# Softmax row sums on VectorE over a pair of heads, and one head of a pair normalised on ScalarE

## The chip, the core and the metric

The kernel runs on one core of a Trainium2 chip. The core has five engines that run their own instruction queues in order and wait for each other by semaphores: TensorE (PE; its weight loads are listed as PEld), VectorE (DVE), ScalarE (ACT), GpSimd (POOL) and SyncE (SP), which here issues nearly all DMAs. The metric is the device time of one execution in microseconds. Three runs of the kernel before took 858.59, 859.97 and 860.6 us; the median is 859.97.

## The reference

Attention feeds two feed-forward layers, all in float32.

```python
def _attn_ref(q, k, v):                       # (4, 8, 576, 64)
    scores = scale * np.matmul(q, k.transpose(0, 1, 3, 2))
    # heads 0-3 see the last 32 keys, heads 4-7 every 32nd key, both causal
    scores = np.where(masks[None, :, :, :], scores, -1e9)
    scores = scores - np.max(scores, axis=-1, keepdims=True)
    attn = np.exp(scores)
    attn = attn / (np.sum(attn, axis=-1, keepdims=True) + 1e-09)
    return np.matmul(attn, v)
# _moe_ref:  h = x @ w_in;  g = s * relu(h)**2 + b;  x = g @ w_out     (2304 x 512 x 2048)
# _moe2_ref: h = x @ w_in;  g = h * cos(h);          x = g @ w_out
```

## The kernel before, in words

**Attention.** The heads of a batch are taken in pairs. A batch has five pairs: two of local heads (kind "loc"), two of strided heads ("str"), and one ("rem") that holds the rows left over from all of them. With four batches there are 20 pairs of two items each, 40 items. A local item has its scores in one PSUM bank as 128 rows by 4 blocks of 96 columns, a strided item as 126 by 4 blocks of 126; a rem item has one block of 96 and two of 72. Softmax runs per row and block, so the statistics of an item are 4 columns (or 1 and 2) of a small tile `sm`: row 0 the negated maximum, row 1 the sum, row 2 its reciprocal. `part` is one large SBUF array; a ring of six pieces of 512 columns in it holds the exponentials p and the transposed p.

For a pair `run_scores` issues the score matmuls, then by a generator: `mask_max` for each item (in batches 0 and 1 PE adds the mask, `PE_MASK = 2`; later VectorE adds it, line 431, and the scores then lie in SBUF), `exps` (line 449: one ACTIVATE per block with a per-row bias, and with `accum_out`, which leaves the row sum), and `norm` on VectorE (lines 462 to 464: add 1e-9, reciprocal, multiply). Each ACTIVATE with `accum_out` shows in the trace as two instructions, ACTIVATE and ACTIVATION_READ_ACCUMULATOR. `run_transp` then transposes p on PE and copies it out on ScalarE (line 482), `run_values` multiplies by V (line 552) and splits the result into a high part (ScalarE, line 133) and a low part (VectorE, line 136), `xhi` and `xlo`, which the first layer reads.

**Order.** The generators are advanced by `tick()`. Batch 0 is done first, with dummy matmuls filling PE (line 531) and weight conversion (lines 143 and 174 to 181 on VectorE, 141 on ScalarE, then the split in lines 133 and 136) between. Then the slots of the first layer run, 20 slots of 512 (or 256) tokens by 4 feature blocks to a pass, and the attention of batches 1 to 3 is issued between them at rates of 0.5 and 0.3 steps to a group of matmuls. A scheduler then places each engine's instructions by their priority and by when it expects their operands. A slot needs the `xhi` and `xlo` of its tokens. The second layer follows, then the output.

Of the kernel before, what the change touches and what calls it, by code (L numbers as in the profile page):

```python
# [103 lines left out]
def net(ctx, tc, qk, rqk, vloc, vstr, rv, w1, w2, s, b, out):  # L104
# [270 lines left out]
    class Item:  # L375


        def __init__(self, bb, hp, j, kind):
# [45 lines left out]
        def mask_max(self, alloc):  # L424
            self.p = alloc()
            self.sm = sm_p.tile([P, 3, 4], F32, tag="sm", name="sm")
            for i, (m, k, n, c, mask) in enumerate(self.parts):
                src = self.view(self.s_ps, i)
                if not self.pe_mask:
                    dst = self.view(self.p, i)  # L430
                    nc.vector.tensor_tensor(dst, src, mask, ALU.add)  # L431
                    src = dst
                nc.vector.tensor_reduce(self.sm[:m, 0, i : i + n], src, axis=AX.X, op=ALU.max, negate=True)  # L433
                nc.vector.tensor_scalar(self.sm[:m, 0, i : i + n], self.sm[:m, 0, i : i + n], SCALE, None, ALU.mult)

# [21 lines left out]

        def norm(self):
            for i, (m, k, n, c, _) in enumerate(self.parts):
                dst = self.view(self.p, i)  # L460
                sm = self.sm[:m, :, i : i + n]
                nc.vector.tensor_scalar_add(sm[:, 1, :], sm[:, 1, :], 1e-9)
                nc.vector.reciprocal(sm[:, 2, :], sm[:, 1, :])
                normed[0] = nc.vector.tensor_tensor(  # L464
                    dst, dst, sm[:, 2, :].unsqueeze(2).to_broadcast([m, n, k]), ALU.mult
                )
# [765 lines left out]
```

## Time and profile before

| | |
|---|---|
| median of three runs | 859.97 us |
| span of the profiled execution, first to last instruction | 858.2 us |
| PE busy | 848.4 us, 99% |
| DVE busy | 594.5 us, 69% |
| ACT busy | 510.3 us, 59% |
| granted TensorE clock, mean | 0.999 of full speed |

For the profiled execution only its span is listed, no time of its own. Busy time of PE is not PE at its peak, since matmuls are pipelined and their ends are modelled. The 40 slices of the page show VectorE and ScalarE busy mainly in the first sixth of the span: the tenths of the first seven slices are 5, 9, 9, 8, 9, 9, 7 for DVE and 6, 8, 8, 9, 8, 9, 7 for ACT, and 3 to 8 thereafter. That sixth holds the attention.

### The profile page before, as it was taken

What the parts mean: (1) busy time and instruction counts of PE and PEld (TensorE: products, weight loads), DVE (VectorE), ACT (ScalarE), POOL (GpSimd) and SP (SyncE); (2) the same over time, 40 slices, a digit from 0 to 9 for tenths busy, and PEclk for the clock granted to TensorE, in tenths of its full rate; (3) what the DMA queues carried; (4) which work ended last, traced back from release to release, by engine and by line L of the source; (5) the groups of instructions that cost most, each with busy time, mean ns of one, the idle gap of its engine ahead of it and who ended that gap; (6) DMA issues with size and microseconds to landing.
All of it is one profiled execution on the core that took longest, in us unless ns stands there. A gap on an engine that the chain in (4) does not pass through costs nothing.

```text
span 858.2 us, 13480 instructions
## 1 busy us (share of the span) xinstructions
PE 848.4 (99%) x4901; PEld 724.5 (84%) x4901; DVE 594.5 (69%) x1269; ACT 510.3 (59%) x1121; POOL 4.0 (0%) x15
## 2 busy tenths in 40 slices
PE   9999999999999999999999999999999999999997
PEld 5667778898888888898888998998988989989886
DVE  5998997379867988597895476555665554644553
ACT  6889897466545765466564566455564554644543
POOL 1000000000000000000000000000000000000000
PEclk9999999999999999999999999999999999999999
DMA  9656551036434755277442765565664655755411
GB/s 282 192 168 181 161 162 50 1 129 202 166 117 147 234 183 175 108 262 254 153 155 86 240 207 179 183 210 172 238 215 160 220 164 183 277 175 189 166 50 75
DMA packets 65203, 147.40 MB, mean 172 GB/s; under 512 B 6272, under 2 KB 24960, under 8 KB 65136
## 3 DMA queue, kind: packets, MB, share of 16 engines
q1 hardware_dynamic: 64992, 146.40, 51.1%
q8 instruction: 39, 0.64, 0.3%
q14 instruction: 28, 0.23, 0.1%
q10 hardware_dynamic: 144, 0.13, 0.0%
HBM read 118.72 MB, written 27.79 MB: 171 GB/s over the span
## 4 chain that ended last, share of the span: by engine, by line
PE 90%; DVE 4%; ACT 4%; DMA 1%; issue 0%; SPq 0%; ACTq 0%
PE acc L1063 23%; PE acc L687 21%; PE h_ps L687 21%; PE pa L1125 10%; PE pb L1125 10%; ACT part L449 2%; PE t_ps L474 1%; PE o_ps L552 1%; DMA wraw<-in_w_dram 1%; PE s_ps L517 1%; DVE part L464 1%; ACT part L482 1%; PE dummy L786 1%; DVE sm L433 0%; ACT xhi L133 0%; DVE part L431 0%
## 5 line engine op out<-in xcount | busy, mean ns | idle before, releaser
L687 PE MATMUL h_ps<-xhi,w 128*128 128x512 f32 (+1 forms) x640 | 197.7, 372 | 0.8 <-ACT xhi L133 0.5
L687 PE MATMUL acc<-gh,w 128*128 128x512 f32 (+1 forms) x640 | 195.9, 370 | 0.0
L1063 PE MATMUL acc<-w2l,gh 128*128 128x512 f32 x576 | 177.7, 390 | 0.0
L687 PEld LDWEIGHTS h_ps<-xhi,w 128*128 128x128 f32 x640 | 116.8, 189 | 22.2 <-DVE w L136 1.0
L136 DVE TENSOR_TENSOR gl<-r,gh 128x512 fp32r<-128x512 f32 (+3 forms) x130 | 96.8, 745 | 53.7 <-ACT gh L998 40.4
L687 PEld LDWEIGHTS acc<-gh,w 128*128 128x128 f32 x640 | 117.0, 189 | 19.9 <-issue 0.2
L1063 PEld LDWEIGHTS acc<-w2l,gh 128*128 128x128 f32 x576 | 107.8, 188 | 21.6
L687 PE MATMUL acc<-gl,w 128*128 128x512 f32 (+1 forms) x320 | 118.5, 370 | 0.0
L687 PE MATMUL h_ps<-xlo,w 128*128 128x512 f32 (+1 forms) x320 | 118.4, 370 | 0.0
L1063 PE MATMUL acc<-w2l,gl 128*128 128x512 f32 x288 | 112.4, 391 | 0.0
L1125 PE MATMUL pa<-xhi,wfl 128*128 128x384 f32 x336 | 99.6, 337 | 0.0
L1125 PE MATMUL pb<-xhi,wfl 128*128 128x384 f32 x336 | 99.5, 336 | 0.0
L710 ACT ACTIVATE r<-h_ps 128x512 f32<-128x512 f32 (+1 forms) x80 | 44.4, 555 | 89.5 <-PE h_ps L687 89.3
L998 ACT ACTIVATE r<-h 128x768 f32<-128x768 f32 (+1 forms) x50 | 40.7, 816 | 95.3 <-DVE h L1111 95.1
L133 ACT ACTIVATE gh<-r 128x512 fp32r<-128x512 f32 (+1 forms) x80 | 47.1, 588 | 39.1 <-DVE r L716 38.7
L687 PEld LDWEIGHTS acc<-gl,w 128*128 128x128 f32 x320 | 60.4, 189 | 9.9
L687 PEld LDWEIGHTS h_ps<-xlo,w 128*128 128x128 f32 x320 | 60.4, 189 | 9.6
L1063 PEld LDWEIGHTS acc<-w2l,gl 128*128 128x128 f32 x288 | 54.1, 188 | 11.2
L1125 PEld LDWEIGHTS pa<-xhi,wfl 128*128 128x128 f32 x336 | 62.0, 188 | 1.7
L1125 PEld LDWEIGHTS pb<-xhi,wfl 128*128 128x128 f32 x336 | 61.9, 188 | 1.5
L1013 ACT ACTIVATE r<-r 128x768 f32<-128x768 f32 (+1 forms) x50 | 40.9, 820 | 32.1 <-DVE r L1011 32.1
L1011 DVE SCALAR_TENSOR_TENSOR r<-a,r 128x768 f32<-128x768 f32 (+1 forms) x50 | 46.2, 926 | 19.6 <-ACT a L998 19.4
(109 smaller groups left out, 1243.0 us busy)
## 6 DMA issues: line engine op xcount, KB each, us to landing
wfl<-wf SPq DMA_DIRECT2D x72, 512.0 KB, 4.9
w2l<-w2s SPq DMA_DIRECT2D x48, 512.0 KB, 3.2
wraw<-in_w_dram SPq DMA_DIRECT2D x56, 256.0 KB, 3.7
praw<-in_w_dram SPq DMA_DIRECT2D x32, 256.0 KB, 3.1
oraw<-in_w_dram SPq DMA_DIRECT2D x16, 512.0 KB, 3.7
wf<-ob SPq DMA_DIRECT2D x16, 512.0 KB, 3.5
w2s<-ow SPq DMA_DIRECT2D x16, 512.0 KB, 3.9
wfl<-wf SPq DMA_DIRECT2D x24, 256.0 KB, 4.1
```

Source lines behind the costliest of these rows:

```text
L133: nc.scalar.activation(dst_hi, src, AF.Copy)
L136: return nc.vector.tensor_tensor(dst_lo, src, hi.bitcast(F32), ALU.subtract)
L449: nc.scalar.activation(dst[:, t, :], src[:, t, :], AF.Exp, bias=self.sm[:m, 0, i + t : i + t + 1], scale=SCALE, accum_out=self.sm[:m, 1, i ...
L464: normed[0] = nc.vector.tensor_tensor(dst, dst, sm[:, 2, :].unsqueeze(2).to_broadcast([m, n, k]), ALU.mult)
L474: self.moves = nc.tensor.transpose(self.t_ps[:k, o : o + m], src[:, t, :], ident[:m, :m])
L687: nc.tensor.matmul(*args, **kw)
L710: relu[0] = nc.scalar.activation(r, h, AF.Relu)
L998: nc.scalar.activation(*args, **kw)
L1011: nc.vector.scalar_tensor_tensor(r, m, MAGIC, r, ALU.subtract, ALU.subtract)
L1013: nc.scalar.activation(r, r, AF.Sin, scale=-TWO_PI)
L1063: nc.tensor.matmul(accs[e], g[:, e * P : (e + 1) * P], w[:, wi, :], start=p == 0 and f == 0 and i == 0, stop=p == NPAIR - 1 and f == 1 and ...
L1125: nc.tensor.matmul(pb[bi], a, b[:, m, :], start=st and m == 0 and i == 0, stop=m == 1 and i == 2, skip_group_check=True)
```

## The change

`accum_out` goes from the exponentials. A new class `Softmax` works on one item ("half") or on both items of a pair, whose p now lie side by side in one piece of 1024 columns and whose statistics share one tile. In batch 0 each item is a half: its row sums come from a TENSOR_REDUCE on VectorE, and VectorE normalises both items as before. In batches 1 to 3 the pair is taken jointly: one maximum where VectorE has added the mask, one scaling, one sum, one addition of 1e-9 and one reciprocal for both items. Item 0 is then normalised on VectorE and item 1 on ScalarE, by one ACTIVATE (Copy with a per-row scale) per block, in one step of the generator later. The ring of pieces is 3 of 1024 columns instead of 6 of 512. The lines of the changed kernel are: 438 exponentials, 534 and 538 maxima, 536 mask, 539 scaling, 543 sums, 544 and 545 addition and reciprocal, 552 the multiplication on ScalarE, 559 that on VectorE, 458 the copy of the transposed p, 758 and 759 the first layer's activation (710 and 711 before).

```diff
@@ exps
                     nc.scalar.activation(
-                        dst[:, t, :],
-                        src[:, t, :],
-                        AF.Exp,
-                        bias=self.sm[:m, 0, i + t : i + t + 1],
-                        scale=SCALE,
-                        accum_out=self.sm[:m, 1, i + t : i + t + 1],
+                        dst[:, t, :], src[:, t, :], AF.Exp, bias=self.sm[:m, 0, i + t : i + t + 1], scale=SCALE
                     )
@@ tevac
-            self.pt = alloc()
+            if self.pt is None:
+                b = alloc()
+                self.pt, self.mate.pt = b[:, :512], b[:, 512:]
@@ new class Softmax
+        def maxima(self):
+            for i, (m, k, n, c, mask) in enumerate(self.parts):
+                for it in self.its:
+                    src = it.view(it.s_ps, i)
+                    if self.pe_mask:
+                        nc.vector.tensor_reduce(it.sm[:m, 0, i : i + n], src, axis=AX.X, op=ALU.max, negate=True)
+                    else:
+                        nc.vector.tensor_tensor(it.view(it.p, i), src, mask, ALU.add)
+                if not self.pe_mask:
+                    nc.vector.tensor_reduce(self.col(i, 0), self.view(i), axis=AX.X, op=ALU.max, negate=True)
+                nc.vector.tensor_scalar(self.col(i, 0), self.col(i, 0), SCALE, None, ALU.mult)
+
+        def sums(self):
+            for i in range(len(self.parts)):
+                nc.vector.tensor_reduce(self.col(i, 1), self.view(i), axis=AX.X, op=ALU.add)
+                nc.vector.tensor_scalar_add(self.col(i, 1), self.col(i, 1), 1e-9)
+                nc.vector.reciprocal(self.col(i, 2), self.col(i, 1))
+
+        def scaled(self, j):
+            it = self.its[j]
+            for i, (m, k, n, c, _) in enumerate(self.parts):
+                dst = it.view(it.p, i)
+                for t in range(n):
+                    nc.scalar.activation(dst[:, t, :], dst[:, t, :], AF.Copy, scale=it.sm[:m, 2, i + t : i + t + 1])
+            it.ready = True
+
+        def norm(self, j):
...
@@ run_scores
-        for it in pair:
-            it.mask_max(alloc)
+        p = alloc().rearrange("p (j c) -> p j c", j=2)
+        sm = sm_p.tile([P, 3, 8], F32, tag="sm", name="sm").rearrange("p r (j n) -> p r j n", j=2)
...
+        if pair[0].bb:
+            both = Softmax(pair, p, sm, 0, 2)
+            both.maxima()
+            yield
+            for it in pair:
+                it.exps()
+                yield
+            both.sums()
+            both.norm(0)
+            yield
+            both.scaled(1)
+            return
+        halves = [Softmax(pair, p, sm, j, j + 1) for j in range(2)]
+        for half in halves:
+            half.maxima()
         yield
         for it in pair:
             it.exps()
             yield
-        for it in pair:
-            it.norm()
-            it.ready = True
+        for half in halves:
+            half.sums()
+            half.norm(0)
@@ alloc
-            o = NP0 + (self.ni % NPB) * 512
+            o = NP0 + (self.ni % (NPB // 2)) * 1024
```

The change moves instructions. First place: VectorE in batch 0, behind the maxima of the first two local pairs. Before, `sm_202` and `sm_205` are the statistics of the two items of the first pair, `sm_232` and `sm_235` those of the second, `sm_318` those of an item of the third.

```order
L434 TENSOR_SCALAR sm_232<-sm_232 128x4
L462 TENSOR_SCALAR sm_202<-sm_202 128x4
L434 TENSOR_SCALAR sm_235<-sm_235 128x4
L463 RECIPROCAL sm_202<-sm_202 128x4
L464 TENSOR_TENSOR part_94<-part_94,sm_202 128x384
L462 TENSOR_SCALAR sm_205<-sm_205 128x4
L463 RECIPROCAL sm_205<-sm_205 128x4
L433 TENSOR_REDUCE sm_318<-s_ps_306 126x4
L464 TENSOR_TENSOR part_94<-part_94,sm_205 128x384
```
In the changed kernel `sm_202` is the first pair's tile and `sm_231` the second's.

```order
L543 TENSOR_REDUCE sm_202<-part_94 128x4
L539 TENSOR_SCALAR sm_231<-sm_231 128x4
L543 TENSOR_REDUCE sm_202<-part_94 128x4
L544 TENSOR_SCALAR sm_202<-sm_202 128x4 x2
L543 TENSOR_REDUCE sm_231<-part_94 128x4
L545 RECIPROCAL sm_202<-sm_202 128x4 x2
L544 TENSOR_SCALAR sm_231<-sm_231 128x4
L559 TENSOR_TENSOR part_94<-part_94,sm_202 128x384 x2
L545 RECIPROCAL sm_231<-sm_231 128x4
```
Three sums (line 543) now stand where the first item's normalisation stood, and both multiplications of the first pair stand together behind the third sum, which belongs to the second pair.

Second place: VectorE at the first two local pairs of batch 2, where VectorE adds the mask. Before, `sm_1033` and `sm_1037` are the first pair's items, `sm_1128` and `sm_1132` the second's.

```order
L462 TENSOR_SCALAR sm_1033<-sm_1033 128x4
L431 TENSOR_TENSOR part_94<-s_ps_1110,mloc_89 128x384
L463 RECIPROCAL sm_1033<-sm_1033 128x4
L431 TENSOR_TENSOR part_94<-s_ps_1111,mloc_89 128x384
L464 TENSOR_TENSOR part_94<-part_94,sm_1033 128x384
L462 TENSOR_SCALAR sm_1037<-sm_1037 128x4
L433 TENSOR_REDUCE sm_1128<-part_94 128x4
L463 RECIPROCAL sm_1037<-sm_1037 128x4
L433 TENSOR_REDUCE sm_1132<-part_94 128x4
L464 TENSOR_TENSOR part_94<-part_94,sm_1037 128x384
L434 TENSOR_SCALAR sm_1128<-sm_1128 128x4
L434 TENSOR_SCALAR sm_1132<-sm_1132 128x4
```
In the changed kernel `sm_1036` is the first pair's tile and `sm_1130` the second's.

```order
L536 TENSOR_TENSOR part_94<-s_ps_1112,mloc_89 128x384
L536 TENSOR_TENSOR part_94<-s_ps_1113,mloc_89 128x384
L176 SCALAR_TENSOR_TENSOR wtmp_2074<-wraw_2069,wtmp_2074 128x256
L538 TENSOR_REDUCE sm_1130<-part_94 128x8
L543 TENSOR_REDUCE sm_1036<-part_94 128x8
L539 TENSOR_SCALAR sm_1130<-sm_1130 128x8
L764 TENSOR_SCALAR r_1259<-r_1259,sb_91 128x512
L544 TENSOR_SCALAR sm_1036<-sm_1036 128x8
L181 SCALAR_TENSOR_TENSOR wtmp_2074<-wraw_2069,wtmp_2074 128x256
L545 RECIPROCAL sm_1036<-sm_1036 128x8
L176 SCALAR_TENSOR_TENSOR wtmp_2074<-wraw_2071,wtmp_2074 128x256
L559 TENSOR_TENSOR part_94<-part_94,sm_1036 128x384
```
Both masks and the joint maximum of the second pair now stand ahead of the first pair's joint sum, and one multiplication is left of two.

Third place: ScalarE over the same two pairs; before, line 449 are the exponentials of both.

```order
L449 ACTIVATE part,sm<-part,sm 128x96 x7
L710 ACTIVATE r<-h_ps 128x512
L711 ACTIVATE r<-r 128x512
L449 ACTIVATE part,sm<-part,sm 128x96 x4
L482 ACTIVATE part<-t_ps 96x512 x2
L449 ACTIVATE part,sm<-part,sm 128x96 x4
L133 ACTIVATE gh<-r 128x512
L133 ACTIVATE xhi<-o_ps 128x512
```
In the changed kernel line 438 are the exponentials and line 552 the multiplications of item 1.

```order
L438 ACTIVATE part<-part,sm 128x96 x8
L758 ACTIVATE r<-h_ps 128x512
L759 ACTIVATE r<-r 128x512
L438 ACTIVATE part<-part,sm 128x96 x4
L552 ACTIVATE part<-part,sm 128x96 x4
L438 ACTIVATE part<-part,sm 128x96 x4
L458 ACTIVATE part<-t_ps 96x512 x2
L133 ACTIVATE gh<-r 128x512
L552 ACTIVATE part<-part,sm 128x96 x4
L133 ACTIVATE xhi<-o_ps 128x512
```
Four multiplications of the first pair stand between the second pair's two groups of exponentials, and four of the second pair's stand ahead of the split of an attention result (`xhi`).

## Rows read from the trace of the kernel before

**Rows 1.** Windows of core 0: start:end and length, busy us (instructions) of each engine, clock, DMA

```profile
7.50:36.60 29.10, 28.00 (x342) 19.44 (x341) 26.10 (x84) 23.17 (x105) 0.00 (x0) 1.00 0.82 248
36.60:69.00 32.40, 30.93 (x286) 23.19 (x286) 29.85 (x107) 28.61 (x103) 0.00 (x0) 1.00 0.58 178
69.00:118.00 49.00, 47.59 (x491) 36.65 (x487) 45.97 (x148) 44.62 (x168) 0.00 (x0) 1.00 0.53 165
118.00:142.00 24.00, 23.79 (x191) 18.94 (x190) 22.62 (x75) 21.10 (x73) 0.00 (x0) 1.00 0.32 100
142.00:200.00 58.00, 58.00 (x315) 49.64 (x314) 34.41 (x84) 31.49 (x67) 0.00 (x0) 1.00 0.24 75
```

**Rows 2.** Chain of waits inside 36.6 to 69 us, shares by line

```profile
by line: DMA wraw<-in_w_dram 29.7%; DVE part L464 11.5%; DVE w L136 7.4%; PE h_ps L687 6.6%; DVE wtmp L176 6.4%; DVE wtmp L181 6.3%; ACT part L449 5.0%; DVE wtmp L143 4.5%; DVE wtmp L174 4.0%; ACT part L482 3.3%; PE t_ps L474 2.7%; DVE xlo 
```

**Rows 3.** Chain of waits inside 69 to 118 us, shares by line

```profile
by line: ACT part L449 29.3%; ACT part L482 10.5%; DVE part L431 8.1%; DVE part L464 7.7%; DVE sm L433 6.7%; ACT xhi L133 5.1%; DVE xlo L136 5.1%; PE t_ps L474 5.0%; PE acc L687 3.9%; issue 2.5%; DVE sm L462 2.2%; ACT w L133 2.1%; PE o_ps L
```

**Rows 4.** Groups by form, ScalarE, 0 to 150: line, shapes, count; busy us, mean ns; idle

```profile
L449 ACT ACTIVATE part<-part,sm 128x96 f32<-128x96 f32 x36 | 13.1, 371 | 1.0 <-DVE sm L434 0.9
...
L449 ACT ACTIVATE part<-part,sm 126x126 f32<-126x126 f32 x32 | 12.4, 394 | 1.5 <-DVE sm L434 1.5
...
L133 ACT ACTIVATE w<-wtmp 128x512 fp32r<-128x512 f32 x13 | 8.4, 643 | 0.4 <-DVE wtmp L181 0.4
...
L714 ACT ACTIVATE r<-r,sb 128x512 f32<-128x512 f32 x4 | 3.3, 832 | 0.1
```

**Rows 5.** Timeline, ScalarE: start us, duration us, engine, line, operation

```profile
108.03 0.38 ACT L449 ACTIVATE part<-part,sm 128x96 f32<-128x96 f32 x1
108.30 0.20 ACT L449 ACTIVATION_READ_ACCUMULATOR part<-part,sm 128x1 f32 x1
108.39 0.37 ACT L449 ACTIVATE part<-part,sm 128x96 f32<-128x96 f32 x1
```

**Rows 6.** Timeline, ScalarE, copies without a pointer operand

```profile
280.20 0.30 ACT L133 ACTIVATE oa<-ta 128x128 fp32r<-128x128 f32 x1
280.40 0.62 ACT L133 ACTIVATE w<-wtmp 128x512 fp32r<-128x512 f32 x1
```

**Rows 7.** Groups by form, VectorE, 0 to 150 us

```profile
L464 DVE TENSOR_TENSOR part<-part,sm 126x504 f32<-126x504 f32 x16 | 10.8, 677 | 0.1
...
L136 DVE TENSOR_TENSOR w<-wtmp,w 128x512 fp32r<-128x512 f32 x13 | 8.8, 680 | 0.8 <-ACT w L133 0.8
...
L433 DVE TENSOR_REDUCE sm<-part 126x4 f32<-126x504 f32 x8 | 5.2, 668 | 0.0
...
L464 DVE TENSOR_TENSOR part<-part,sm 72x144 f32<-72x144 f32 x8 | 2.4, 298 | 0.0
...
L464 DVE TENSOR_TENSOR part<-part,sm 128x96 f32<-128x96 f32 x8 | 2.0, 249 | 0.0
...
L433 DVE TENSOR_REDUCE sm<-part 72x2 f32<-72x144 f32 x4 | 1.1, 282 | 0.0
...
L433 DVE TENSOR_REDUCE sm<-part 128x1 f32<-128x96 f32 x4 | 1.0, 240 | 0.0
```

**Rows 8.** Timeline, VectorE, 75.3 to 76.8 us

```profile
75.34 0.54 DVE L433 TENSOR_REDUCE sm<-part 128x4 f32<-128x384 f32 x1
75.80 0.16 DVE L463 RECIPROCAL sm<-sm 128x4 f32<-128x4 f32 x1
75.88 0.52 DVE L433 TENSOR_REDUCE sm<-part 128x4 f32<-128x384 f32 x1
76.32 0.54 DVE L464 TENSOR_TENSOR part<-part,sm 128x384 f32<-128x384 f32 x1
76.79 0.23 DVE L434 TENSOR_SCALAR sm<-sm 128x4 f32<-128x4 f32 x2
```

**Rows 9.** Waits of VectorE, 7.5 to 150 us: total us, times, longest us

```profile
DVE sm L462 <- ACT part L449: 3.9, 9, 1.4
```

More of the change, by code (lines that the diff above doesn't have):

```diff
@@ L380, in __init__ @@
             self.ready = self.moved = self.stored = False
+            self.pt = self.mate = None
             if kind == "loc":
@@ L422, in view @@
             return t[:m, c : c + n * k].rearrange("p (n k) -> p n k", k=k)
[L424 to L434, printed above, removed]
         def run_transp(self, tag, alloc):
@@ L449, in exps @@
                     nc.scalar.activation(
-                        dst[:, t, :],
-                        src[:, t, :],
-                        AF.Exp,
-                        bias=self.sm[:m, 0, i + t : i + t + 1],
-                        scale=SCALE,
-                        accum_out=self.sm[:m, 1, i + t : i + t + 1],
-                    )
[L458 to L466, printed above, removed]
+                        dst[:, t, :], src[:, t, :], AF.Exp, bias=self.sm[:m, 0, i + t : i + t + 1], scale=SCALE
+                    )
         def transp(self, tag):
@@ L533, in fill, with __init__, view, col @@
                 )
+    class Softmax:
+        def __init__(self, pair, p, sm, lo, hi):
+            self.its = pair[lo:hi]
+            self.pe_mask = pair[0].pe_mask
+            self.parts = pair[0].parts
+            self.p = p[:, lo:hi, :]
+            self.sm = sm[:, :, lo:hi, :]
+        def view(self, i):
+            m, k, n, c, _ = self.parts[i]
+            return self.p[:m, :, c : c + n * k].rearrange("p j (n k) -> p j n k", k=k)
+        def col(self, i, r):
+            m, _, n, _, _ = self.parts[i]
+            return self.sm[:m, r, :, i : i + n]
+        def maxima(self):
[22 more added lines that the diff above has]
+        def norm(self, j):
+            it = self.its[j]
+            for i, (m, k, n, c, _) in enumerate(self.parts):
+                dst = it.view(it.p, i)
+                normed[0] = nc.vector.tensor_tensor(
+                    dst, dst, it.sm[:m, 2, i : i + n].unsqueeze(2).to_broadcast([m, n, k]), ALU.mult
+                )
+            it.ready = True
@@ L535, in run_scores @@
     def run_scores(pair, tag, pe_mask, alloc):
         pair_scores(pair, tag, pe_mask)
-        for it in pair:
-            it.mask_max(alloc)
+        p = alloc().rearrange("p (j c) -> p j c", j=2)
+        sm = sm_p.tile([P, 3, 8], F32, tag="sm", name="sm").rearrange("p r (j n) -> p r j n", j=2)
+        for j, it in enumerate(pair):
+            it.p, it.sm = p[:, j, :], sm[:, :, j, :]
+        if pair[0].bb:
[10 more added lines that the diff above has]
+            return
@@ L599, in __init__ @@
                 self.pairs.append([Item(bb, None, j, "rem") for j in range(2)])
+            for a, b in self.pairs:
+                a.mate, b.mate = b, a
             self.n = 0
@@ L605, in alloc @@
         def alloc(self):
-            o = NP0 + (self.ni % NPB) * 512
+            o = NP0 + (self.ni % (NPB // 2)) * 1024
             self.ni += 1
-            return part[:, o : o + 512]
+            return part[:, o : o + 1024]
         def pair(self, q):
```

## The prediction

> **What bounds the kernel now.** I read the windows first. From 142 us on PE is busy in every microsecond while VectorE and ScalarE have over 40% of their time free [rows 1]; nothing of the attention is left there, and what the change gives or costs earlier passes through to the end unaltered. Between 7.5 and 142 us the three engines are all nearly full: VectorE 26.1 of 29.1 us in the stretch of batch 0, 29.85 of 32.4 and 45.97 of 49 in the next two, ScalarE 23.17, 28.61 and 44.62 [rows 1]. There a microsecond of extra work on either has little room. Then I read which of them the chain of waits runs through. From 36.6 to 69 us 29.7% of it is the flight of weight blocks and 40% six lines of VectorE; ScalarE has 8.3%, exponentials and copies of transposed p together [rows 2]. From 69 to 118 us it changes hands: exponentials 29.3%, copies of transposed p 10.5%, splits 5.1% and 2.1%, together 47% on ScalarE, and some 30% in five VectorE lines [rows 3]. From 118 us on PE is the fullest engine (23.79 of 24 us) [rows 1].
>
> The sum is made against the profiled execution's span of 858.2 us. The median of the runs shown, 859.97 us, lies 1.8 us above that span; the trace lists nothing around the span, so I add the difference to the median.
>
> **What an exponential gives up.** One exponential of 96 columns starts 0.27 us before its accumulator read, and the read holds the queue for 0.09 us until the next one starts [rows 5]. So the sure saving is 0.09 us each. It could be more if the read waits for the exponential to drain: a plain 128-column copy starts its follower after 0.20 us [rows 6], which would make the saving 0.36 - 0.20 = 0.16 us. Against the second reading stands the price of pointer operands: a 512-column ACTIVATE with per-row scale and bias takes 832 ns, one without 643 ns [rows 4], about 0.095 us for each pointer. An exponential has one, the plain copy none; 0.20 less a little for fewer columns plus 0.095 gives back the 0.27. I take 0.09 us.
>
> The Trainium skill, page "ScalarE: Activation LUTs", section "What ACT_TABLE_LOAD costs", states the same thing as a rule: a per-partition pointer adds about 93 ns to an ACTIVATE, and neighbours overlap by about that much. As an estimate it gives 360 ns for the 96-column exponential (the trace has 371) and a pace of 267 ns; by it the first reading holds and the multiplication put on ScalarE, which has a pointer too, is no cheaper than an exponential.
>
> **ScalarE.** Batch 0 has 38 exponentials (2 x 2 x 4 local, as many strided, 6 rem): 38 x 0.09 = 3.4 us less. Batches 1 to 3 have 114: 10.3 us less. They gain one multiplication per block of item 1, 57 in all, at the pace of an exponential without its read: 0.27 us local, 0.29 strided (23 ns longer) [rows 4], 0.25 for 72 columns. A batch has 8 x 0.27 + 8 x 0.29 + 0.27 + 2 x 0.25 = 5.3 us, three have 15.8. Net +5.5 us, 1.8 per batch. The bounds: at the plain pace of 0.20 us the exponentials save 18.2 and the multiplications cost 11.4, net -6.8; with no overlap (0.38 us) [rows 4] they cost 21.7, net +11.4.
>
> **VectorE, batch 0.** It gains a sum per item. A reduce of 384 columns holds the queue 0.46 us (75.34 to 75.80) [rows 8], one of 504 lasts 0.668 [rows 7] and so holds 0.59; rem 0.16 and 0.20 by the same subtraction. That is 4 x 0.46 + 4 x 0.59 + 2 x 0.36 = 4.9 us; nothing goes. The stretch has 29.1 - 26.1 = 3.0 us of VectorE idle [rows 1]. If all of it fills, the stretch grows by 1.9 us; if none, by 4.9. Part of that idle time is VectorE standing in `L462` for the end of exponentials (nine waits, 3.9 us, some of them later) [rows 9], and ScalarE is 3.4 us lighter here, so I take the low end. At the end of the stretch the last step of a weight conversion (0.68 us alone, 0.60 in a queue) [rows 7] has moved from in front of the last `xlo` to behind it, which takes it off the way to the first slot: +1.3 us, with 4.3 as the upper bound. The first pair's first multiplication comes later, behind three sums (first place of the order); I charge nothing for that by itself, because the second pair's exponentials, which those sums wait for, also end earlier by 16 x 0.09 us. Without that cover it would cost up to the 0.46 us of the third sum.
>
> **VectorE, batches 1 to 3.** The fixed part of a reduce, from 96 and 504 columns (0.240 and 0.668) [rows 7], is 0.14 us with 1.05 ns a column, so a joint sum holds 0.87 us local, 1.12 strided, and 0.26 and 0.36 rem. Away go one multiplication (0.47 local [rows 8]; 0.60 strided, 0.18 and 0.23 rem [rows 7]) and one each of scaling, addition and reciprocal, which hold 0.08 us (75.80 to 75.88) and last 0.16 [rows 8]; for rem these are six. Local: +0.15 to -0.09; strided +0.28 to +0.04; rem -0.27 to -0.75. A batch: +0.59 to -0.85. In batches 2 and 3 the joint maximum saves the fixed part less overlap, 0.4 a batch. In all +1.0 to -3.4 us; I take -1.0, near the middle, since these small steps are partly filled and partly chained.
>
> **What of it lies on the path.** From 69 to 118 us ScalarE has about half of the chain, so of batches 2 and 3 (3.7 us) half counts: +1.8. Batch 1 falls where ScalarE has a twelfth of it: +0.2. Of VectorE's -1.0 a third: -0.3. Sum: 1.3 + 1.8 + 0.2 - 0.3 = +3.0 us, so **863.0 us**. Behind the waiting instructions stand others: in ScalarE's queue the split of an attention result now waits behind four multiplications of the next pair (third place of the order); they need that pair's joint sum, and PE waits for the split only at the next batch's tokens.
>
> **Rivals.** *A, faster:* the accumulator read drains the exponential, and ScalarE's net is -6.8 us. This decides where the pace without the read is under 0.24 us, since 114 x (0.36 - p) = 57 x p there. Half of 4.5 and a twelfth of 2.3 give -2.4; VectorE's nine waits shrink by half, -2; batch 0 stays +1.3: -3.1 us, 856.9. For it speaks that the exponentials head the chain from 69 us on; against it the pointer's price. *B, no change:* VectorE goes to its low bound (-3.4, a third of it on the path) and half of ScalarE's +2.0 falls into its idle time: 1.3 + 1.0 - 1.1 = +1.2, 861.2. For it speaks that ScalarE idles 3.8 and 4.4 us in the two stretches [rows 1]; against it that this idle time comes in waits which the fixed order does not fill. *C, slower by more:* a joint sum needs both items' exponentials, so VectorE's queue stands at fifteen places for a whole pair, with the next pair's scaling and a weight step behind it (second place of the order). At the mean wait, 3.9/9 = 0.43 us [rows 9], that is 6.5 us; with half of the old waits gone, about +4.5 on top of batch 0: 866. Against it: in that place two masks and a maximum now stand ahead of the sum and give the exponentials time.
>
> **Numbers.** Forecast 0.41, A 0.25, B 0.23, C 0.11. A measurement of this kernel tells about 0.2% (1.7 us) from no change. A and a little of B make faster 0.26; B and the edge of the forecast 0.24 same; the rest of the forecast and C 0.50 slower. The likeliest case alone spans 861.7 to 865. The range for eight in ten runs from A's time to C's and a little beyond, which also takes in most of batch 0's upper bound (4.3 for 1.3): 856.5 to 867.
>
> **What would show it.** ACTIVATION_READ_ACCUMULATOR gone from the groups; exponentials of 96 columns following each other at 0.27 us (rival A: 0.20), the multiplications of line 552 likewise; ScalarE busier from 36.6 to 118 us by some 5 us; the joint sums at 0.95 us; the first slot's long run of matmuls 1 to 2 us later; waits of VectorE for line 438 no longer in sum than 3.9 us (C: above 6). I am wrong if the stretch from 69 to 118 us becomes shorter, or if PE is full from before 142 us on without a gap.

## The result, and the profile after

The changed kernel takes 867.91 us (median of four, 867.01 to 871.46) against 859.85 us for the kernel before: a ratio of 1.0102, 95% interval 1.008 to 1.0123. It is 8.1 us slower, where I forecast 3.0, and lies above the range. The profiled execution spans 866.8 us, 8.6 more than before.

The windows of the changed kernel, in the order of [rows 1] (window, length, then busy us and instructions of PE, weight loads, DVE, ACT, POOL; granted clock, DMA share, GB/s):

```profile
7.50:36.60 29.10, 26.84 (x329) 17.66 (x321) 27.28 (x89) 17.80 (x54) 0.00 (x0) 1.00 0.87 249
36.60:69.00 32.40, 26.96 (x224) 19.56 (x224) 27.98 (x75) 25.27 (x75) 0.00 (x0) 0.95 0.46 138
69.00:118.00 49.00, 47.87 (x461) 36.69 (x459) 42.14 (x111) 43.48 (x125) 0.00 (x0) 1.00 0.52 151
118.00:142.00 24.00, 23.45 (x218) 18.12 (x218) 20.89 (x50) 21.05 (x61) 0.00 (x0) 1.00 0.48 144
142.00:200.00 58.00, 58.00 (x356) 48.88 (x356) 37.74 (x97) 37.28 (x93) 0.00 (x0) 1.00 0.23 69
```

From 36.6 us to 142 us VectorE and ScalarE are busy for less time than before [rows 1], and yet the kernel is slower. Read the first busy column instead. PE has idle time of 2.26, 5.44, 1.13 and 0.55 us in the first four stretches, 9.38 in all; before it was 1.10, 1.47, 1.41 and 0.21, in all 4.19 [rows 1]. That is 5.2 us more, 4.0 of it in one stretch, 36.6 to 69 us, and 1.2 in batch 0. In the same row the granted clock is 0.95: PE ran part of the stretch at the lower of its two levels, 1.2 GHz, and 32.4 x 0.05 is 1.6 us lost. Idle time and clock make 6.8 of the 8.6 us. The rest does not show as idle: a busy PE is not PE at its peak.

The prices of the single instructions came out as forecast (line, engine, operation, shapes, count; busy us, mean ns of one; idle before):

```profile
L438 ACT ACTIVATE part<-part,sm 128x96 f32<-128x96 f32 x36 | 10.4, 365 | 0.8 <-DVE sm L539 0.7
L552 ACT ACTIVATE part<-part,sm 128x96 f32<-128x96 f32 x26 | 7.8, 364 | 0.5 <-DVE sm L539 0.5
L543 DVE TENSOR_REDUCE sm<-part 126x8 f32<-126x1008 f32 x6 | 7.2, 1200 | 3.9 <-ACT part L438 3.9
L543 DVE TENSOR_REDUCE sm<-part 128x8 f32<-128x768 f32 x6 | 5.7, 952 | 4.0 <-ACT part L438 4.0
```

An exponential lasts 365 ns (371 before [rows 4]), a multiplication on ScalarE as much, and the joint sums 0.95 us (forecast 0.95) and 1.20. ACTIVATION_READ_ACCUMULATOR is gone. The pace shows where the trace lists a run of equal instructions as one (start, duration of the run, count at the end):

```profile
109.03 1.26 ACT L552 ACTIVATE part<-part,sm 126x126 f32<-126x126 f32 x4
110.20 0.63 ACT L438 ACTIVATE part<-part,sm 128x96 f32<-128x96 f32 x2
```

Two exponentials take 0.63 us, so the second starts 0.63 - 0.365 = 0.27 us behind the first, as forecast. Four strided multiplications take 1.26, a pace of (1.26 - 0.39) / 3 = 0.29. These read SBUF. In batches 0 and 1 the exponentials read PSUM and follow each other faster; the kernel before has there:

```profile
8.75 0.34 ACT L449 ACTIVATE part<-s_ps,sm 128x96 f32<-128x96 f32 x1 [6.52 <-DVE sm L434]
8.98 0.19 ACT L449 ACTIVATION_READ_ACCUMULATOR part<-s_ps,sm 128x1 f32 x1
9.08 0.33 ACT L449 ACTIVATE part<-s_ps,sm 128x96 f32<-128x96 f32 x1
```

That is 0.33 us from one to the next, 0.10 of it for the read; fifteen of the changed kernel (the run at 39.31 us further down) take 3.59 us, a pace of (3.59 - 0.34) / 14 = 0.23. So the read's 0.09 to 0.10 us is what went, in all batches, and no price of an instruction failed. What grew are the waits (engine, line, tile, who is waited for; total us, times, longest us), to be held against [rows 9]:

```profile
DVE sm L543 <- ACT part L438: 8.4, 10, 1.8
DVE xlo L136 <- ACT xhi L133: 6.0, 11, 1.7
ACT xhi L133 <- PE o_ps L598: 5.9, 7, 1.5
```

VectorE stands 8.4 us in front of sums for the exponentials, ten times, where it stood 3.9 us in all [rows 9]. That is rival C's mark ("above 6"). But look where these waits are; the same view from 36.6 to 69, 69 to 118 and 118 to 150 us:

```profile
DVE sm L543 <- ACT part L438: 0.8, 2, 0.6
DVE sm L543 <- ACT part L438: 3.2, 3, 1.8
DVE sm L543 <- ACT part L438: 4.0, 3, 1.7
```

7.2 us of them lie behind 69 us, in batches 2 and 3, where PE loses nothing to speak of: its idle time from 69 to 142 us is 1.68 us, for 1.62 before. In the stretch in which PE's idle time grew by 4.0 us they are 0.8 us. The chains of waits, from 36.6 to 69 us (in place of [rows 2]) and from 69 to 118 us (in place of [rows 3]):

```profile
by line: DMA wraw<-in_w_dram 24.3%; ACT part L438 9.2%; DVE sm L543 9.1%; PE o_ps L598 8.1%; PE acc L735 6.3%; DVE wtmp L176 5.2%; DVE sm L534 5.0%; DVE part L559 4.4%; DVE wtmp L143 4.1%; DVE xlo L136 4.0%; DVE wtmp L181 3.9%; DVE w L136 3
by line: PE h_ps L735 10.5%; ACT part L438 10.0%; PE acc L735 9.6%; PE t_ps L448 7.7%; ACT part L552 7.2%; PE o_ps L598 6.4%; DVE sm L543 5.5%; DVE xlo L136 5.4%; ACT xhi L133 5.2%; DVE sm L538 4.0%; ACT part L458 3.3%; ACT gh L133 3.2%; is
```

In the first the exponentials have risen from 5.0% to 9.2%, and behind them stand the new sums with 9.1% and two lines of PE. In the second ScalarE no longer has 47%: its exponentials fell from 29.3% to 10.0%, and PE's lines lead. The softmax did not do this. A kernel with the changed layout alone (e6 below), which takes the time of the kernel before, has from 69 to 118 us:

```profile
by line: ACT part L441 12.1%; PE h_ps L748 10.1%; DVE part L540 8.7%; DVE sm L542 8.4%; PE t_ps L452 8.0%; DVE part L564 7.3%; PE acc L748 6.5%; PE o_ps L611 5.8%; ACT part L462 5.7%; DVE xlo L139 5.1%; issue 3.4%; PE s_ps L497 3.2%; DVE w 
```

Its exponentials (line 441 there) have 12.1%. The shares in this stretch move that far while the time stands still, so they are no measure of what a microsecond on ScalarE costs.

The new way of a pair is seen at the first pair of batch 1 (start, duration, engine, line; in brackets the idle time just before, and who ended it):

```profile
39.31 3.59 ACT L438 ACTIVATE part<-s_ps,sm 128x96 f32<-128x96 f32 x15
41.31 0.95 DVE L543 TENSOR_REDUCE sm<-part 128x8 f32<-128x768 f32 x1 [0.59 <-ACT part L438]
42.51 0.20 DVE L545 RECIPROCAL sm<-sm 128x8 f32<-128x8 f32 x1
42.81 1.18 ACT L552 ACTIVATE part<-part,sm 128x96 f32<-128x96 f32 x4
44.11 0.58 ACT L758 ACTIVATE r<-h_ps 128x512 f32<-128x512 f32 x1
45.26 1.06 ACT L458 ACTIVATE part<-t_ps 96x512 f32<-96x512 f32 x2
46.37 1.15 PE L598 MATMUL o_ps<-part,v 96*64 96x64 f32 x32 [1.27 <-ACT part L458]
```

The run of fifteen holds the pair's eight exponentials and seven of the next pair. VectorE waits 0.59 us for the last exponential of item 1; from the start of the joint sum to the reciprocal's end pass 1.40 us; then ScalarE multiplies, with the next pair's exponentials and a first-layer activation around it in its queue; then it copies the transposed p, and PE has stood 1.27 us.

How one late wait passes through all engines is seen between 57 and 70 us. First VectorE, ScalarE and PE (columns as above):

```profile
57.73 0.68 DVE L136 TENSOR_TENSOR xlo<-o_ps,xhi 128x512 fp32r<-128x512 f32 x1
60.30 0.29 DVE L143 TENSOR_SCALAR wtmp<-wraw 128x256 f32<-128x256 f32 x1 [1.89 <-DMA wraw<-in_w_dram]
60.51 1.27 DVE L534 TENSOR_REDUCE sm<-s_ps 126x4 f32<-126x504 f32 x2
62.55 2.16 ACT L438 ACTIVATE part<-s_ps,sm 126x126 f32<-126x126 f32 x8 [3.73 <-DVE sm L539]
63.73 0.65 PE L448 MATMUL t_ps<-ident,part 126*126 126x126 f32 x4 [1.94 <-ACT part L438]
```

VectorE waits 1.89 us for a weight block, with the next pair's maxima queued behind it; so ScalarE waits 3.73 us for the maxima, and PE 1.94 us for the exponentials. Then the windows around that gap:

```profile
61.50:63.70 2.20, 0.29 (x2) 0.00 (x0) 2.20 (x9) 1.15 (x5) 0.00 (x0) 1.00 0.49 185
63.70:64.60 0.90, 0.87 (x6) 0.83 (x7) 0.78 (x3) 0.90 (x5) 0.00 (x0) 1.00 0.73 141
64.60:68.30 3.70, 3.70 (x24) 2.52 (x22) 3.39 (x8) 2.47 (x6) 0.00 (x0) 0.54 0.30 91
```

PE is busy 0.29 of 2.20 us; 0.9 us later its clock falls, and for 3.70 us it works at a mean of 0.54 of full speed, though it is busy in all of them. That costs 3.70 x 0.46 = 1.7 us on top of the gap. The Trainium skill, page "TensorE: Matmul & The Clock Gate", section "HAM oscillation — how this bites in real kernels", describes this: idle gaps drop the clock, and the throttled time costs half its length. The trace agrees: here a gap stands ahead of the fall, and in half-microsecond windows the fall lost 1.71 us. Other falls in these runs came without such a gap (last section).

### The profile page after: what moved, and what is told of

It is laid out like the page before. It is cut to its first block, busy times and chain, and to the rows that moved or that the text cites. A ratio compares the mean times of both kernels' runs of the same rounds, so it can differ in the third digit from the quotient of the medians.

```text
span 866.8 us, 13345 instructions
## 1 busy us (share of the span) xinstructions
PE 851.8 (98%) x4901; PEld 724.5 (84%) x4901; DVE 600.4 (69%) x1215; ACT 512.0 (59%) x1026; POOL 4.0 (0%) x15
## 4 chain that ended last, share of the span: by engine, by line
PE 89%; DVE 5%; ACT 4%; DMA 1%; issue 0%; ACTq 0%; DVEq 0%
PE acc L1111 23%; PE acc L735 21%; PE h_ps L735 20%; PE pb L1173 10%; PE pa L1173 10%; ACT part L438 2%; PE o_ps L598 2%; PE t_ps L448 1%; DVE sm L543 1%; DMA wraw<-in_w_dram 1%; ACT xhi L133 1%; DVE xlo L136 1%; PE s_ps L493 1%; PE dummy L834 1%; ACT part L552 1%; DVE sm L534 1%
```

## The experiments

All kernels but the changed one run from one source, where three constants choose, per batch, accumulators, the joint form, and the item normalised on ScalarE. The changed kernel is this setting:

```diff
+ACC = ()                      # batches with accum_out, and without sums on VectorE
+JOINT = (1, 2, 3)             # batches that take the pair as one
+SCALED = {1: 1, 2: 1, 3: 1}   # batch: item that ScalarE normalises
```

Each diff below is against it unless it names another kernel. Where a batch isn't joint, each item has its own maximum, sum, reciprocal and multiplication. Differences are medians against the runs of the kernel before made on the same chip (859.43 to 859.84 us). e18 sums 8 columns of each block and leaves out the rest, so it serves for timing only.

| run | what it is | median, us | difference | ratio, 95% |
|---|---|---|---|---|
| e6 | layout only | 860.30 | +0.5 | 0.9999 to 1.0016 |
| e2 | batch 0 only | 863.85 | +4.1 | 1.0042 to 1.007 |
| e17 | e6, batch 0's sums done beside the chain | 866.28 | +6.4 | 1.0063 to 1.0088 |
| e18 | e2 with short sums | 861.47 | +1.6 | 1.0007 to 1.0025 |
| e12 | e2, one item on ScalarE | 867.43 | +7.8 | 1.0073 to 1.01 |
| e16 | e2, maxima first | 872.97 | +13.5 | 1.0136 to 1.0165 |
| e1 | batches 1 to 3 only | 866.62 | +6.9 | 1.0067 to 1.0093 |
| e13 | batches 2 and 3 only | 860.52 | +1.1 | 1.0004 to 1.0022 |
| e14 | batch 1 only | 863.45 | +4.0 | 1.0034 to 1.0064 |
| e3 | e1, both items on VectorE | 862.46 | +2.7 | 1.0019 to 1.0043 |
| e4 | e1 with accumulators | 866.23 | +6.5 | 1.0066 to 1.0091 |
| e8 | e4, both items on VectorE | 864.75 | +4.9 | 1.0051 to 1.0079 |
| e11 | e8, maxima by item | 861.84 | +2.2 | 1.0009 to 1.0031 |
| e9 | e3, by item | 861.57 | +2.0 | 1.0017 to 1.004 |
| e10 | e9, one item on ScalarE | 863.35 | +3.7 | 1.0027 to 1.0053 |
| e5 | after, late weight moved | 867.15 | +7.3 | 1.0075 to 1.0101 |
| e7 | after, item 0 on ScalarE | 865.65 | +5.8 | 1.0054 to 1.008 |
| e15 | e4, idle time filled | 865.47 | +6.0 | 1.0058 to 1.0082 |

### Which part costs: batch 0, and batches 1 to 3

```diff
# e1
+ACC = (0,)
# e2
+ACC = (1, 2, 3); JOINT = (); SCALED = {}
# e6
+ACC = (0, 1, 2, 3); JOINT = (); SCALED = {}
```

e1: 

> Batch 0 sums by ScalarE's accumulators as before the change, batches 1 to 3 as changed. Handover theory (the 8 us come mostly from batches 1 to 3, where a pair's chain now crosses between VectorE and ScalarE twice behind in-order queues, and from one late weight block at 60 us): 864 to 866, so 4 to 6 us stay. Batch 0 theory (the sums added in batch 0 and what they push later cost most): 861 to 862. Work theory (the forecast's: ScalarE's extra work of 5.5 us at half weight): 861.5.

e2: 

> Batch 0 as changed, batches 1 to 3 with accumulators and both items normalised on VectorE as before. Handover theory: 862 to 863, the 2.8 us by which batch 0 ends later. Batch 0 theory: 866 or more. Work theory: 861.2.

e6: 

> Only the changed layout (both items of a pair side by side, shared statistics tile, three pieces of 1024): accumulators in all batches, both items normalised on VectorE one by one. Every theory of cost by work or handover: 859.2 to 860.4, as before. If the new order of instructions by itself costs something (other places for weight steps), 861 to 862.

The layout costs 0.5 us, within what can be told. Batch 0 alone costs 4.1 us, batches 1 to 3 alone 6.9 (each with the layout); together 8.1, so they overlap by 3. e1 rules out the batch 0 theory and the work theory, and is a little above the handover theory (866.62 for 864 to 866); e2 lies between the handover theory and the batch 0 theory. So there are two costs, and neither has the forecast's size.

### Batches 2 and 3, or batch 1

```diff
# e13
+ACC = (0, 1); JOINT = (2, 3); SCALED = {2: 1, 3: 1}
# e14
+ACC = (0, 2, 3); JOINT = (1,); SCALED = {1: 1}
```

e13: 

> The change in batches 2 and 3 alone (joint sums, item 1 on ScalarE); batches 0 and 1 with accumulators and item by item on VectorE. Idle theory (the price of a later pair is TensorE's idle time, and TensorE has none to lose behind 69 us, where it has slots of the first layer to do): 859.8 to 861. Work theory (ScalarE holds half of the chain there; the forecast put 1.8 of its 2.0 us of batches 1 to 3 here): 861.5 to 864, and the larger part of the 6.9.

e14: 

> The change in batch 1 alone. Idle theory: nearly all of the 6.9 us of batches 1 to 3, 864.5 to 867, with 3 us or more of additional TensorE idle time between 36.6 and 69 us and a fall of the granted clock. Work theory: +0.2 by the forecast's term, 860 to 861.

The windows of e13 (36.6 to 69, 69 to 118, 118 to 142 us), then of e14 (36.6 to 69, and a gap in it):

```profile
36.60:69.00 32.40, 30.75 (x286) 22.95 (x285) 29.75 (x103) 28.49 (x99) 0.00 (x0) 1.00 0.59 176
69.00:118.00 49.00, 48.30 (x444) 36.62 (x443) 42.22 (x108) 41.14 (x123) 0.00 (x0) 1.00 0.51 153
118.00:142.00 24.00, 23.53 (x213) 18.49 (x212) 19.54 (x42) 21.82 (x61) 0.00 (x0) 1.00 0.34 99
```

```profile
36.60:69.00 32.40, 28.02 (x226) 20.68 (x227) 28.10 (x77) 26.94 (x77) 0.00 (x0) 0.95 0.53 153
60.50:63.00 2.50, 0.62 (x5) 0.62 (x6) 2.47 (x9) 1.81 (x8) 0.00 (x0) 1.00 0.57 174
```

In batches 2 and 3 the change costs 1.1 us, 0.5 of it the layout. There PE's idle time even falls (0.70 us from 69 to 118 us, for 1.41 before [rows 1]). The attention does run later: the splits of batch 3's results start 6.5 to 10.1 us after those of before, and VectorE's waits in front of joint sums are as long as in the changed kernel. But PE does first-layer slots meanwhile. The waits of e13 from 69 to 150 us, and then the first layer's matmuls alone from 69 to 118 us, before (line 687) and in e13 (line 748; PE, weight loads, clock, DMA share, GB/s):

```profile
DVE sm L548 <- ACT part L441: 8.5, 5, 3.0
69.00:118.00 49.00, 30.37 (x111) 19.66 (x111) 1.00 0.53 165
69.00:118.00 49.00, 35.29 (x128) 23.04 (x127) 1.00 0.51 153
```

So 8.5 us of waits of VectorE for line 441 come with 1.1 us of cost. Batch 1 alone costs 4.0 us, with 4.38 us of idle PE from 36.6 to 69 us for 1.47 before, and the clock at 0.95; the fall came at 37 us, ahead of the gap shown. Its six runs reach from 861.5 to 865.7, with mean clocks from 1.000 down to 0.997: whether the clock falls is not the same in each run, but the clock alone does not order them (865.7 at 0.998, 862.9 at 0.997). The idle theory holds; the amount is a little below what it expected (864.5). e13 and e14 together make 5.1 us of e1's 6.9; why the two cost more together is not shown.

### Batch 0: work or chain

```diff
# e17, against e6
             half.norm(0)
+            if bb == 0:
+                for i in range(len(half.parts)):
+                    nc.vector.tensor_reduce(half.col(i, 0), half.view(i), axis=AX.X, op=ALU.add)
# e18, against e2
-nc.vector.tensor_reduce(self.col(i, 1), self.view(i), axis=AX.X, op=ALU.add)
+nc.vector.tensor_reduce(self.col(i, 1), self.view(i)[:, :, :, 0:8], axis=AX.X, op=ALU.add)
-1e-9
+1e-9 if self.its[0].bb else 1.0
# e12, against e2
+SCALED = {0: 1}
# e16, against e2
+with tc.high_priority() if bb == 0 else nullcontext():
     half.maxima()
```

e17: 

> Accumulators and normalisation as before in all batches (new layout), and in batch 0 VectorE does the sums as well, behind each item's multiplication, where nothing needs them: the 4.9 us of work without the chain. Work theory (batch 0 costs because VectorE has 4.9 us more to do): 862.5 to 865. Chain theory (it costs because reciprocal and multiplication wait for the sum, and the sum for the exponentials, in VectorE's queue): 860 to 861.5.

e18: 

> Batch 0 without accumulators as changed, but its sums cover only the first 8 columns of each block (and 1.0 is added in place of 1e-9): the chain stays, most of the work goes, about 0.15 us for a sum instead of 0.46 to 0.59; batches 1 to 3 as before. Work theory: 860 to 861.5, since 3.4 of the 4.9 us are gone. Chain theory: 862.5 to 864.5, as with the whole sums.

e12: 

> Batch 0 with sums on VectorE, item 1 of each pair normalised on ScalarE, which is busy 17.8 of 29.1 us there; batches 1 to 3 as before the change. If batch 0 costs by VectorE's added work (4.9 us of sums against 3.0 idle): five multiplications of 0.47 to 0.60 less, 861 to 862. If it costs by the longer chain from exponentials to transposes: 863 to 865.

e16: 

> Batch 0 as changed, batches 1 to 3 as before, and the maxima of batch 0 ordered ahead of the sums wherever both could go. Order theory (batch 0's cost comes from the next pair's maxima standing behind the sums, so that ScalarE and then TensorE wait): 860.5 to 862.5 instead of 863.85. Work theory (4.9 us of sums in a stretch with 3.0 us of idle VectorE): 863.3 to 865.

The windows 7.5 to 36.6 and 36.6 to 69 us, of e17, then of e18:

```profile
7.50:36.60 29.10, 28.05 (x315) 19.79 (x312) 26.12 (x81) 20.34 (x90) 0.00 (x0) 1.00 0.80 246
36.60:69.00 32.40, 28.32 (x247) 20.40 (x244) 29.01 (x98) 25.81 (x97) 0.00 (x0) 0.95 0.49 146
```

```profile
7.50:36.60 29.10, 28.18 (x347) 19.13 (x341) 26.14 (x96) 19.55 (x65) 0.00 (x0) 1.00 0.90 254
36.60:69.00 32.40, 28.98 (x265) 21.83 (x269) 30.21 (x105) 27.15 (x100) 0.00 (x0) 1.00 0.59 178
```

The sums as work beside the chain, which nothing needs, cost 6.4 us, more than either theory expected; the chain with short sums costs 1.6. That speaks for work: less the layout's 0.5 and one fall of the clock (1.7), e17 pays 4.2 of the 4.9 us, e2 less the layout 3.7. The first slot's first matmul shows the same: it starts at 35.85 us with the layout alone, at 36.06 in e18, 38.29 in e2 and 40.46 in e17. That e17 is dearer than e2 I put down to the fall and to the reads that ScalarE keeps; the second no run shows apart. The time is lost from 36.6 us on (4.08 us of idle PE in e17, for 1.47 [rows 1]): what VectorE does later in batch 0 makes the first slots and batch 1 late.

e12 and e16 went against the theories they were made for. Moving five multiplications from VectorE to ScalarE made batch 0 slower, 7.8 for 4.1 us, although ScalarE had the room. Its profile has one fall of the clock, at 32.5 us; the rest I put down to the new step in the middle of the chain, which no run shows by itself. In e16 the priority moved PE's order as well. The scores of batch 1 came ahead of transposes, and PE stood for their keys (PE's timeline, then a window):

```profile
25.16 1.53 PE L497 MATMUL s_ps<-qk 64*64 64x96 f32 x14 [1.82 <-DMA qk<-in_qk_dram]
```

```profile
25.00:38.20 13.20, 12.82 (x74) 8.19 (x75) 5.03 (x13) 1.48 (x5) 0.00 (x0) 0.50 0.47 135
```

After that gap PE worked at 0.50 of its clock for 13.2 us, 6.6 us lost in one stroke, and a second fall at 48.5 us lost 1.7 more. So e16 doesn't tell whether the order of the maxima matters in batch 0.

### Batches 1 to 3: sums, joint form, ScalarE's multiplication

```diff
# e3
+ACC = (0,); SCALED = {}
# e4
+ACC = (0, 1, 2, 3)
# e8
+ACC = (0, 1, 2, 3); SCALED = {}
# e11, against e8
-            both.maxima()
+            for j in range(2):
+                Softmax(pair, p, sm, j, j + 1).maxima()
# e9
+ACC = (0,); JOINT = (); SCALED = {}
# e10
+ACC = (0,); JOINT = ()
# e7
+SCALED = {1: 0, 2: 0, 3: 0}
```

e3: 

> Batch 0 as before; batches 1 to 3 with joint sums on VectorE, but both items normalised on VectorE. ScalarE loses 10.3 us of reads and gains nothing; VectorE gains the sums and loses no multiplication. Handover theory: the second crossing (VectorE's reciprocal to ScalarE's multiplication) is gone, so about 861 to 863. Work theory: VectorE has 6 to 7 us more than before in the stretches where it is nearly full, 863 to 865.

e4: 

> Accumulators in all batches, no sums on VectorE; batches 1 to 3 still joint in maximum, addition and reciprocal, and item 1 normalised on ScalarE. Handover theory: the wait for both items' exponentials and the crossing to ScalarE stay, 863 to 865. Work theory: ScalarE has 15.8 us more than before and VectorE about 9 us less: 863 to 866 if ScalarE bounds.

e8: 

> Accumulators in all batches; batches 1 to 3 joint only in maximum, scaling, addition and reciprocal, both items normalised on VectorE. VectorE loses its small steps, ScalarE is as before. Handover theory: only the wait for both items' exponentials is left, 860 to 861.5. Work theory: VectorE some 2 us lighter, 859 to 859.7.

e11: 

> Accumulators in all batches, both items normalised on VectorE; batches 1 to 3 have maxima item by item as before, and only addition and reciprocal are joint. If the wait of item 0 for item 1's exponentials is what the joint form costs: 864 to 865, as with the maxima joint too. If it is the joint maximum (the first exponential waits for both items' masks): 860 to 861.

e9: 

> Batch 0 as before; in batches 1 to 3 no accumulators, but each item keeps its own maximum, sum, reciprocal and multiplication on VectorE, item by item as before the change. Joint theory (taking the pair as one costs 4 to 5 us, since item 0 then waits for item 1's exponentials; the relief of ScalarE by the reads gives some 2 back): 857 to 859. Work theory (VectorE carries 15 sums for 3 batches of both items more and drops nothing): 862 to 865, above the 862.5 with joint sums.

e10: 

> As the kernel with sums item by item, but item 1 of each pair is normalised on ScalarE. Joint theory: ScalarE waits only for item 1's own sum; 859 to 862. Handover theory (the normalisation on ScalarE costs by itself, 1.5 to 4 us): 861 to 864.

e7: 

> The changed kernel, but item 0 goes to ScalarE and item 1 to VectorE in batches 1 to 3. TensorE transposes item 1 first there, so item 1 no longer waits for ScalarE. Handover theory: 2 to 4 us of the 8 come back, 864 to 866. Work theory: the same work, 867.5 to 868.5.

Three readings. First, ScalarE's work by itself does not set the time. Between 7.5 and 142 us e4 keeps ScalarE busy for 121.95 us and e1 for 112.34, and they take the same time (+6.5, +6.9). VectorE has the sums less in e4 (104.44 us busy for 116.35), so a gain there may hide a cost here; no run parts the two. Second, joining the pair costs without adding any work: e8 only merges small steps of VectorE, and is 4.4 us slower than the layout alone; the work theory had it below before. Its profile has 3.38 us of idle PE from 36.6 to 69 us, for 1.76 with the layout alone. 2.7 of the 4.4 us comes with the joint maximum and scaling (e8 for e11), 1.7 with the joint addition and reciprocal (e11 for the layout). Third, ScalarE's multiplication costs on top: 4.2 us with joint sums (e1 for e3), 1.6 with accumulators (e4 for e8), 1.8 item by item (e10 for e9), of which only the first is clear of the intervals in the table. With sums item by item and no work on ScalarE (e9) 2.0 us are left, between what the joint theory and the work theory expected. e4 and e8 came out above both of their figures, e11 between, e3, e7 and e10 in the range of the handover theory. e7 gives back 2.3 of the 8.1: TensorE transposes item 1 first, and as the handover theory had it, it is better that this one doesn't wait for ScalarE.

The clock runs through all of these steps. Of the profiled runs e1, e3, e7, e8 and e9 have one fall, e4 two, e10 and e11 none, at 1.71 us each; and a median need not have the fall of its profile. The four runs of e9 at a mean clock of 0.999 to 1.000 took 861.2 to 861.6 us, the two at 0.997 863.2. By the runs at 0.999 to 1.000 alone e8 takes 864.0 to 864.3, so the joint form's cost is not the clock's: it is 3.7 to 4.0 us above the layout alone without it. e10 by the same rule takes 861.4 and 862.2, hardly more than e9; and all five runs of e4 have the clock of two falls (0.995). So with accumulators, or item by item, the price of ScalarE's multiplication may be the clock's alone.

### The late weight block, and the clock

```diff
# e5: maxed[0] is the scaling of the maxima of the fourth pair of batch 1
-            ops.append(lambda t=t, h=hi32: rebias(t, h, on_act))
+            def first(t=t, h=hi32):
+                with tc.issue_after(maxed[0].ins) if key == (3, 0) and maxed[0] is not None else nullcontext():
+                    rebias(t, h, on_act)
+            ops.append(first)
# e15, against e4
         pv_pair(i0, it, o)
+        if it.bb == 0 and it.kind == "rem":
+            fill(4, tail[0])
```

e5: 

> The changed kernel with one difference: the first conversion step of weight block (3, 0) is ordered behind the maxima of the fourth pair of batch 1, so that VectorE no longer waits for that block's DMA at 60 us with the maxima behind it. Late block theory (that wait of 1.9 us left PE idle for 2.1 us and then at half clock for 3.7 us, 4.0 us together): 863.5 to 864.5, no half clock between 60 and 70 us. Rival (the pairs behind are late anyway, for the handovers between VectorE and ScalarE, and PE idles later instead): 866.5 to 868.

e15: 

> The kernel with accumulators and item 1 on ScalarE (866.23), with four dummy matmuls behind the last value matmuls of batch 0 and nothing else moved: they fill some of TensorE's idle time at 37 us, ahead of the fall of the granted clock at 37.5 us. Clock theory (that fall costs 1.71 us of itself and follows from the idle time before it): 864 to 865.2, only the fall at 51 us left. Rival (the fall is a consequence of what comes later, or the dummies cost as much as they save): 866 to 867.

Windows of e5: 36.6 to 69 us, a place that was not touched, and the place of the gap:

```profile
36.60:69.00 32.40, 29.15 (x240) 21.02 (x241) 29.11 (x78) 26.95 (x78) 0.00 (x0) 0.95 0.53 153
40.30:44.00 3.70, 3.70 (x11) 2.87 (x10) 2.94 (x9) 3.70 (x17) 0.00 (x0) 0.54 0.56 174
60.00:66.00 6.00, 5.67 (x45) 4.13 (x43) 5.30 (x17) 4.16 (x13) 0.00 (x0) 1.00 0.79 242
```

The gap at 61.5 us is gone, and its fall of the clock; PE's idle time in the stretch is 3.25 us for 5.44. But the median moved by 0.8 us only, within the intervals, as the rival expected. Not quite for its reason: PE does not stand idle later instead, but in this profile the clock falls at 40.3 us, at the end of batch 0, and takes 1.7 us of what was won. So the late block by itself is worth under 1 us here; whether it would be worth more without the other fall, the run does not tell.

For e15 the windows 36 to 37.5 and 37.5 to 41.3 us, first of e4 without the dummies, then with them:

```profile
36.00:37.50 1.50, 0.94 (x15) 0.74 (x15) 1.50 (x3) 1.41 (x8) 0.00 (x0) 1.00 0.09 11
37.50:41.30 3.80, 3.54 (x9) 2.62 (x9) 1.95 (x9) 3.80 (x24) 0.00 (x0) 0.55 0.90 285
```

```profile
36.00:37.50 1.50, 1.50 (x19) 0.99 (x19) 1.50 (x4) 1.41 (x8) 0.00 (x0) 1.00 0.16 17
37.50:41.30 3.80, 3.47 (x15) 2.37 (x15) 1.95 (x9) 3.80 (x23) 0.00 (x0) 1.00 0.89 305
```

Four matmuls that compute nothing fill the first window (1.50 us busy for 0.94), and the clock stays at 1.00 in the second (0.55 without them). The kernel gains 0.8 us (0.5 against its own runs of before, within the intervals) of the fall's 1.71; the fall at 51 us stays. Where the rest goes is not shown. The expected 864 to 865.2 was too low by a little.

No version beat the kernel before. PE's idle time between 7.5 and 142 us there is 4.19 us [rows 1], so relief of the other engines had at most that to give.

## Why the prediction was wrong

- **The bound.** "There a microsecond of extra work on either has little room" was right for batch 0 and wrong as a way to count. From 36.6 us on the cost was mainly what PE stood idle, and what its clock lost: 6.8 of 8.6 us in the profile with batch 0's share. "Nothing of the attention is left there" was nearly right for the time from 142 us on: before, the last split of a result starts at 143.40 us.
- **Prices.** Right: the read's 0.09 us, the pace of 0.27 and 0.29 us, the joint sums of 0.95 us, ScalarE's multiplications. Rival A fell with them. Its mark, a pace under 0.24 us, is met where exponentials read PSUM (0.23), but there the pace with the read was 0.33, not the 0.36 that the mark was worked out from; the read gave 0.10 us.
- **Batch 0, +1.3.** This term failed by its size: it took the low end of its bounds. Batch 0 alone measured +4.1 (3.7 without the layout), near the upper bound of 4.3, and e17 and e18 say that it is mainly the work. "I charge nothing" for the later multiplication did not decide it (e18: the chain with short sums costs 1.6, 1.1 without the layout).
- **What lies on the path, batches 1 to 3.** This step failed in kind. It shared out engine time by shares of the chain of waits, and so put +1.8 on batches 2 and 3 and +0.2 on batch 1. Measured, each less the layout: about 0.6 for batches 2 and 3 (e13), 3.6 for batch 1 (e14). And the share itself was no property of the stretch: with the layout alone the exponentials have 12.1% for 29.3, in the same time. A share of the chain says who is late where something is late; it doesn't say whether PE has other work. Behind 69 us it had (e13 does 17 matmuls of the first layer more by 118 us). From 36.6 to 69 us the changed kernel does fewer (15.58 us, 53 of them, for 19.17 us and 70 before). I read this as a lack of work: in batch 1 slots of the first 512 tokens are all that PE has besides attention. No run gives it more, so that is argued.
- **VectorE's credit of -0.3** for merged steps had the wrong sign: merged steps alone cost 4.4 us over the layout (e8). That the first item waits for the second explains at most the 1.7 us of e11, which lie within the intervals; the rest comes with the joint maximum and scaling.
- **Rival C** got 0.11, and its mark came (waits of VectorE for line 438 above 6 us; measured 8.4). That its 866 lies nearest is luck all the same: 7.2 us of the waits lie in batches 2 and 3, where 8.5 us of them cost 1.1 us (e13). The counter-argument failed too: masks and a maximum gave the exponentials time at the place it was read from, but behind 69 us VectorE stood up to 1.8 us for them.
- **The first slot's** matmuls started at 39.37 us for 36.57, 2.8 us later, not 1 to 2. **"ScalarE busier from 36.6 to 118 us by some 5 us"** was wrong: 68.75 us for 73.23 [rows 1]. Part of the work moved to later: from 142 to 200 us it is 37.28 us for 31.49 [rows 1]. "PE full from before 142 us without a gap" did not come.
- **Not in the forecast at all**: the fall of the granted clock, 1.71 us each time, which turned a gap of 2 us into nearly 4.

What stays open: why the joint maximum and scaling (e8 for e11) cost 2.7 us, some 2 of it in runs without a fall of the clock. In e8's profile VectorE waits 2.6 us for weight blocks from 36.6 to 69 us, in e11's 0.7, so a moved weight step may have a part in it; no run tests that for e8. Open are also the 1.7 us of the changed kernel that neither idle time nor clock shows. In the other profiles that remainder of the extra span lies between -1.1 and +2.4 us, so idle time and clock tell the time to some 2 us, not better.

## What to carry to other kernels

Where one engine is nearly full, price a change on the others by what it makes that engine stand idle, stage by stage: ask in which stage it has other work to do meanwhile, and how much idle time there is to win at all. Joining two items to save instructions makes the first wait for the second; here the joint form cost 4.4 us where it was to save work. A long wait of a side engine is no cost by itself: 8.5 us of it cost 1.1 us where the full engine had other work. A forecast of a gap of some 2 us on TensorE must allow for the half clock behind it.

## What the runs showed of the hardware

- A single fall of TensorE's clock cost 1.70 to 1.71 us in each profile that has one (after, e1, e3, e5, e7, e8, e9, e12, e14, e15, e17; e4 has two of them, and e16 one beside its long one), with PE busy for nearly all of it in the rows shown. A gap of 1.9 us of idle PE (2.20 us with 0.29 busy) went before one at 64.6 us, but a merely sparse stretch did too: 0.94 us busy of 1.5 in e4.
- The busy share ahead does not tell by itself whether the clock falls: from 36.6 to 40.3 us PE is busy 2.41 of 3.70 us in the changed kernel, with no fall there, and 2.60 in e5, with a fall at 40.3 us.
- The fall is not the same in each run of a kernel: e9's runs had mean clocks of 0.997 (863.2 us) or of 0.999 to 1.000 (861.2 to 861.6 us).
- In e16 PE stayed at half clock for 13.2 us while 12.82 of them were recorded as busy, at first in short matmuls of scores.
- An exponential that reads PSUM has a shorter pace than one that reads SBUF, 0.23 for 0.27 us at 96 columns.
